# Attention with a cached key and value, and a gated mixer: two of seven reads of a product pair on ScalarE, an interleaved order of VectorE's additions, early gating for two quarters

## The chip, the core and the metric

The kernel runs on one core of one Trainium2 chip. A core has five engines that run their own instruction streams in order: TensorE (PE in the profile, with PEld for its weight loads), VectorE (DVE), ScalarE (ACT), GpSimd (POOL) and SyncE (SP), which here issues nearly all DMAs. The engines wait for one another with semaphores. The metric is the time of one execution on the device in microseconds (us); less is better.

## What is computed

The reference layer-normalises `x` (2048 tokens of width 512), runs attention over a cached key and value (32 heads, 2048 keys, head width 128), runs a mixer with an MLP on the same normalised input, and combines them:

```python
xn = _layernorm(x, axis=-1)
q = (xn @ wq).reshape(B, Sq, H, Dh).transpose(0, 2, 1, 3)
scores = jnp.einsum("bhqd,bhkd->bhqk", q, k_cache) * (Dh ** -0.5)
p = _softmax(scores, axis=-1)
s = jnp.einsum("bhqk,bhkd->bhqd", p, v_cache).transpose(0, 2, 1, 3).reshape(B, Sq, H * Dh) @ wo
...
g = _silu(_B_ref(xn, w1, w2, w3, w4))
return x + s * g
```

All inputs and the output are bfloat16. `_B_ref` is a layer norm, a 512x512 product with gelu, a shift of the four column quarters along the tokens, a second 512x512 product added to its input, and an MLP of width 1792.

## The kernel before, in words

A first stage (about 120 us) computes layer norms, the mixer and most of the MLP, and leaves the gate `g` (twice silu's value) in the tile `xall`, 128 tokens by 512 per block. The rest is attention, and the change is all in there.

Attention is cut into 128 units. A unit is one head and one quarter of 512 query tokens; the order is group of four heads (8 groups, `g`), then quarter (`qt`, 4), then head in the group (`hh`, 4). A unit `u` has eight slots (`p` = 0 to 7), so the loop at the end of the function runs over slots `n = 8u + p`, and everything that any engine does is put into a slot by hand; the order of the calls is the order on each engine. In each slot

- `s_slot` makes two score matmuls of 128x512 into one of two PSUM tiles `ps_s`, and one exp of 128x1024 on ScalarE into `pT` (L416);
- `pv_run` makes two matmuls of probabilities and values of the slot ten slots back into `ps_o` (two PSUM banks, one for each unit);
- further matmuls make the query projection of later units (`q_mm` or `product`) and the output projection of earlier ones (`wo_mm` into `ps_wo`, one token block of 128 for about each unit).

The softmax sums need the probabilities of a unit added up over all keys. VectorE does that in bf16: `add_first` (L422) and two `add_next` (L427) add four tiles of 128x2048 into `acc`; `fold` (L431) and `fold_last` (L435) fold it to 128x512. Then `turn` (L460) transposes it with a DMA into `tT`, `turned_sums` reduces it (L465, `sm`) and takes the reciprocal (L467, `rc`), a 2 KB DMA writes that to DRAM (L469, `dr`), `bcast` (L473) reads it back to all partitions with a 256 KB DMA (`rb`), and `norm` (L485) multiplies `ps_o` by `rb` into `oT`, which the output projection reads. In slot terms: the last `add_next` of unit `u-1`, its folds, and `turned_sums` of unit `u-2` stand at `p = 0` of unit `u`; `bcast(u-2)` at `p = 1`; `turn(u-1)` at `p = 3`; `norm(u-2)` at `p = 7`. So the write of `dr` and the read of `rb` for unit `u-2` lie between `p = 0` and `p = 7` of the same unit `u`.

The query projection of units 16 to 125 goes by pairs of heads with a scheme of Strassen's kind: 7 products of half-size blocks (`product`, two matmuls of 128x256 each) in place of 8, put into one PSUM tile `ps_q` with two sides. Products 1, 6 and 2 fill it first; then the same buffer (there is one) takes products 7, 5, 4 and 3. `q_part` takes the results out in four steps, which read PSUM seven times in all: step 0 copies side 0 to `m1` (L388) and adds side 1 to it (L389, `u`); step 1 copies side 0 into the query tile (L392); step 2 adds (L397, then L398, which needs L397's result); step 3 adds `u` to both sides (L400). All are on VectorE. They stand at slots 3, 6, 11 and 14 of 16.

`wo_post` adds a block of the output projection to its sum `sacc` (L549). In the last group the sum is multiplied by the gate (L558) and the input is added (L560). For the last quarter (`LATE = (QT - 1,)`) that is done in advance: once the block's sum of group `GY - 1` is there, `fin_load` loads the input block, `y_scale` (L515) multiplies the sum by the gate, and `y_add` (L520) adds the input, one unit apart; a block that comes later, in group `GY` or after, is multiplied by the gate by itself (`tm`) and added.

On SP's queue all DMAs are issued in program order, and an issue that has to wait (for `dr` to have landed, for example) holds up those behind it.

Of the kernel before, what the change touches and what calls it, by code (L numbers as in the profile page):

```python
# [8 lines left out]
ACT = mybir.ActivationFunctionType  # L9
ALU = mybir.AluOpType  # L10
FP32 = mybir.dt.float32
BF16 = mybir.dt.bfloat16
# [5 lines left out]
def kernel(  # L18
# [15 lines left out]
    nc = tc.nc  # L34
    P = nc.NUM_PARTITIONS
# [9 lines left out]
    QT = Sq // 512  # L45
# [6 lines left out]
    NG = H // HG  # L52
# [9 lines left out]
    pin = tc.keep_in_program_order  # L62
# [28 lines left out]
    qp2 = ent(pool("qp2", 2))  # L91
    smp = ent(pool("smp", 4))
# [18 lines left out]
    def mm(out, lhsT, rhs, start, stop, **kw):  # L111
# [9 lines left out]
        out=ident[:], in0=diag[:], scalar1=0.0, scalar2=None, op0=ALU.is_equal))  # L121
# [1 line left out]
    HEAD = 7  # L123
    XS = 3 * QT + 1
    units = [(g, qt, hh) for g in range(NG) for qt in range(QT) for hh in range(HG)]
    LATE = (QT - 1,)
    GY = NG - 1
    NU = len(units)
    TURN = range(NU - HG)
    NS = NU * SPU  # L130
    kTs, vBs, wqs, wos, oTs, st = {}, {}, {}, {}, {}, {}
# [202 lines left out]
    sw = {}  # L334
# [28 lines left out]
    def product(v, k):  # L363
# [16 lines left out]
        for dc in range(2):  # L380
            mm(s["ps"][:, side, :], b[:, dc, :], x[:, dc, :], k in (1, 7) and dc == 0, True, skip_group_check=True)

    def q_part(v, i):
        s = sw[v]
        ps, t = s["ps"], lambda: pS.tile([P, 256], FP32, tag="tq", bufs=3, name="tq")
        if i == 0:
            m1, s["u"] = t(), t()
            pin(nc.vector.tensor_copy(out=m1[:], in_=ps[:, 0, :]))  # L388
            pin(nc.vector.tensor_tensor(out=s["u"][:], in0=ps[:, 1, :], in1=m1[:], op=ALU.add))  # L389
        elif i == 1:  # L390
            q = s["q"] = qp2.tile([P, 4, 256], BF16, name="qT")
            pin(nc.vector.tensor_copy(out=q[:, 0, :], in_=ps[:, 0, :]))  # L392
            for j in range(2):
                st[v + j] = dict(qT=q[:, 2 * j:2 * j + 2, :].rearrange("d a b -> d (a b)"))
        elif i == 2:
            u3 = t()
            pin(nc.vector.tensor_tensor(out=u3[:], in0=ps[:, 0, :], in1=s["u"][:], op=ALU.add))  # L397
            pin(nc.vector.tensor_tensor(out=s["q"][:, 3, :], in0=ps[:, 1, :], in1=u3[:], op=ALU.add))  # L398
        else:
            pin(nc.vector.tensor_tensor(  # L400
                out=s["q"][:, 1:3, :], in0=ps[:], in1=s["u"][:].unsqueeze(1).to_broadcast([P, 2, 256]),
                op=ALU.add))
            del sw[v]
# [21 lines left out]
    def add_next(u, i):  # L425
        a = st[u]["acc"]
        pin(nc.vector.tensor_tensor(out=a[:], in0=a[:], in1=st[u]["pT"][i][:], op=ALU.add))  # L427

    def fold(u):
        a = st[u]["acc"]  # L430
        pin(nc.vector.tensor_tensor(out=a[:, 0:2, :], in0=a[:, 0:2, :], in1=a[:, 2:4, :], op=ALU.add))  # L431

    def fold_last(u):
        a = st[u]["acc"]
        pin(nc.vector.tensor_tensor(out=a[:, 0, :], in0=a[:, 0, :], in1=a[:, 1, :], op=ALU.add))  # L435
# [25 lines left out]

    def turned_sums(u):
        s = st[u]
        sm = smp.tile([P, 4], FP32, name="sm")
        pin(nc.vector.tensor_reduce(out=sm[:], in_=s["tT"][:], axis=mybir.AxisListType.X, op=ALU.add))  # L465
        rc = smp.tile([P, 4], FP32, name="rc")
        pin(nc.vector.reciprocal(out=rc[:], in_=sm[:]))  # L467
        s["dr"] = drp.tile([P, 4], FP32, name="dr")
        pin(nc.sync.dma_start(out=s["dr"][:], in_=rc[:]))  # L469
# [190 lines left out]
    for jc in range(DC):  # L660
        b = BASE_J[jc]
# [150 lines left out]
    pS = None  # L812
    for h in range(HG):
        load_wo(h)
    for g in range(NG - 1):
        b = (g * QT + QT - 1) * HG
# [45 lines left out]
    UA, UB = NU - 2, NU - 1  # L862
# [14 lines left out]
    steps = defaultdict(list)  # L877
    for v in pairs:
        a = (v - 2) * SPU
        for k, n in ((1, 1), (6, 2), (2, 5), (7, 8), (5, 9), (4, 12), (3, 13)):  # L880
            steps[a + n].append((product, v, k))
        for i, n in enumerate((3, 6, 11, 14)):
            steps[a + n].append((q_part, v, i))

    def run_steps(n, which):
        for fn, v, k in steps.get(n, ()):
            if fn is which:
                fn(v, k)
# [4 lines left out]
    for h in range(HG, H, 2):  # L893
        u = (h // HG) * QT * HG + (-4, -2)[h % HG // 2]
# [8 lines left out]
    for n in range(UB * SPU):  # L903
        u, p = divmod(n, SPU)
        extra = len(wo_todo) > 1 and u in (2 * HG, 2 * HG + 1)
        if p == 0 and wo_box:
            wo_slot(4, n, each=1)
        s_slot(u, p)
        pv_run(n)
        for v, dcs in q_plan.get(n, ()):  # L910
            q_mm(v, dcs)
        run_steps(n, product)
        if p == 0 and u - 2 in TURN:
            turned_sums(u - 2)
        if p == 1 and u - 2 in TURN:
            bcast(u - 2)
        if p == 0 and 1 <= u:
            add_next(u - 1, 3)
            fold(u - 1)
            if u != UA:  # L920
                fold_last(u - 1)
        if p == 3 and u - 1 in TURN:
            turn(u - 1)
        if p == 0:
            twice = extra
        if twice and p < 3:
            wo_slot(p, n, tag="xa")
        for v, k in ((u + 1, 3), (u + 2, 7)):
            if p == k and "psq" in st.get(v, ()) and (k == 3) == (v > FIRST):
                q_copy(v)  # L930
        if p == 3:
            run_steps(n, q_part)
        if u - 2 in TURN:
            norm_p, sum_p, wo_p, each = 7, 5, 3, 1
        else:
            norm_p, sum_p, wo_p, each = 4, 5, 4, 1
        at_wo = [wo_p + i for i in range(HG // each + 1)]
        if FIRST - 2 <= u < LAST:
            at_wo = ([0, 3, 4, 6, 7], [0, 2, 3, 6, 7], [3, 4, 5, 6, 7], [0, 2, 3, 6, 7])[u % 4]
        if p == norm_p and 2 <= u and not u - 2 in TURN:  # L940
            norm_queue(u - 2)
        if p == sum_p and 1 <= u and u - 1 not in TURN:
            sums(u - 1)
        if p == sum_p + 1 and 1 <= u and u - 1 not in TURN:
            bcast(u - 1)
        if u == UA and p in (1, 2, 3):
            wo_slot(p - 1, n)
            if p == 3:
                fold_last(u - 1)
        if p in at_wo and wo_todo and pS is not None and (p == at_wo[0] or wo_box):  # L950
            wo_slot(at_wo.index(p), n, each=each)
        if p == norm_p and u - 2 in TURN:
            norm_queue(u - 2)
        if p != 3:
            run_steps(n, q_part)
        if p == 4:
            add_first(u)
        if p == 6:
            add_next(u, 2)
        pay()  # L960
        held_mm(n)
        for fn in todo.pop(n, ()):
            fn()
        if pS is None and not held:
            right.close()
            pS = right.enter_context(pool("pS", side="right", reuse_waits="tile"))
# [3 lines left out]
    n = UB * SPU  # L970
# [156 lines left out]
```

## Time and profile before

| | |
|---|---|
| median of 3 runs | 1246.01 us (1244.84 to 1246.2) |
| profiled execution, its own time | 1244.64 us |
| its span, first to last instruction | 1242.8 us |
| busy: PE, DVE, ACT | 1230.5, 1081.4, 1092.2 us |
| granted TensorE clock | 1.00 |

A row of a group reads: line, engine, operation, out<-in by the program's names, shapes, count, then busy time, mean ns of one, and the idle time of the engine just before these instructions with what ended it. A row of the timeline reads: start, duration, engine, line, operation, names, count, and in brackets the idle time before it. SPq is SP's queue, whose rows are DMA issues. A busy share of PE is not proof that PE runs at its peak, since matmuls are pipelined and overlap; starts that follow at the least distance are.

### The profile page before, as it was taken

Reading aid. Unit: us, or ns where it says so; the run is one execution under the profiler, and the core shown is the slowest. Engines: PE = TensorE matmul, PEld = TensorE weight load, DVE = VectorE, ACT = ScalarE, POOL = GpSimd, SP = SyncE. Lnnn points to the kernel's source line nnn. Section 1 sums busy time; section 2 is a strip of 40 time slices with the busy share of each in tenths; the row PEclk is TensorE's granted clock in tenths of the full one; section 3 lists DMA queues with packets and bytes.
Section 4 is the critical chain, followed back from the end, with each engine's and each line's share of the span. In section 5 each row is a group of like instructions: output and inputs, shape, how many; then the busy total and the mean of one; then the engine's idle time right before and its main releaser. Section 6 shows DMA issues by size and latency. Waiting matters only on the chain.

```text
span 1242.8 us, 17421 instructions
## 1 busy us (share of the span) xinstructions
PE 1230.5 (99%) x6267; PEld 645.0 (52%) x6267; DVE 1081.4 (87%) x1745; ACT 1092.2 (88%) x1127; POOL 26.8 (2%) x75
## 2 busy tenths in 40 slices
PE   9999999999999999999999999999999999999898
PEld 7444444455555555555555555555555555555445
DVE  7712778899999999999999999999999999999997
ACT  6345999899999999999999999999999999999886
POOL 5300000000000000000000000000000000000000
PEclk9999999999999999999999999999999999999999
DMA  7660123554334524443244423453354433563322
GB/s 176 169 138 31 30 39 65 100 97 88 69 73 106 108 47 85 91 111 77 63 96 98 94 60 82 94 117 61 66 103 94 90 69 74 104 114 68 68 73 82
DMA packets 244055, 107.74 MB, mean 87 GB/s; under 512 B 194816, under 2 KB 227712, under 8 KB 243968
## 3 DMA queue, kind: packets, MB, share of 16 engines
q1 hardware_dynamic: 243408, 106.17, 40.9%
q8 instruction: 49, 0.80, 0.3%
q10 hardware_dynamic: 560, 0.46, 0.1%
q14 instruction: 38, 0.31, 0.1%
HBM read 67.50 MB, written 2.36 MB: 56 GB/s over the span
## 4 chain that ended last, share of the span: by engine, by line
PE 86%; DVE 11%; DMA 2%; ACT 1%; issue 1%; SPq 0%; DVEq 0%; ACTq 0%
PE ps_s L112 35%; PE ps_o L112 33%; PE ps_q L112 7%; PE ps_wo L112 7%; DVE acc L427 3%; PE ps_m L112 2%; DVE oT L485 1%; DVE acc L431 1%; DMA rb<-dr 1%; DVE sm L465 1%; ACT pT L416 1%; DVE sacc L549 1%; DVE xall L558 1%; DVE acc L422 1%; DVE acc L435 1%
## 5 line engine op out<-in xcount | busy, mean ns | idle before, releaser
L416 ACT ACTIVATE pT<-ps_s 128x1024 bf16<-128x1024 f32 x1016 | 1019.7, 1024 | 77.0 <-PE ps_s L112 41.6
L112 PE MATMUL ps_s<-qT,kT 128*128 128x512 bf16 (+1 forms) x2064 | 609.1, 377 | 0.0
L112 PE MATMUL ps_o<-pT,vb 128*128 128x512 bf16 x1984 | 589.9, 379 | 0.0
L427 DVE TENSOR_TENSOR acc<-acc,pT 128x2048 bf16<-128x2048 bf16 x254 | 306.9, 1208 | 11.5 <-ACT pT L416 11.2
L112 PEld LDWEIGHTS <-kT 128*128 128x128 bf16 x2064 | 232.9, 113 | 147.3 <-issue 2.1
L112 PEld LDWEIGHTS <-vb 128*128 128x128 bf16 x1984 | 193.9, 98 | 216.9 <-issue 0.3
L112 PE MATMUL ps_wo<-wo_h,oT 128*128 128x512 bf16 x496 | 186.2, 379 | 0.1
L422 DVE TENSOR_TENSOR acc<-pT 128x2048 bf16<-128x2048 bf16 x127 | 154.8, 1219 | 20.4 <-ACT pT L416 20.1
L431 DVE TENSOR_TENSOR acc<-acc 128x1024 bf16<-128x1024 bf16 x127 | 87.9, 692 | 4.3
L485 DVE TENSOR_TENSOR oT<-ps_o,rb 128x512 bf16<-128x512 f32 x127 | 86.7, 683 | 1.8 <-DMA rb<-dr 1.5
L112 PEld LDWEIGHTS <-oT 128*128 128x128 bf16 x528 | 59.1, 112 | 49.5 <-issue 0.6
L465 DVE TENSOR_REDUCE sm<-tT 128x4 f32<-128x512 bf16 x124 | 84.0, 678 | 0.7 <-DMA tT<-acc 0.7
L549 DVE TENSOR_TENSOR sacc<-ps_wo,sacc 128x512 f32<-128x512 f32 x108 | 73.9, 685 | 0.3 <-PE ps_wo L112 0.3
L112 PEld LDWEIGHTS <-wc 128*128 128x128 bf16 x440 | 43.0, 98 | 58.4 <-issue 8.1
L112 PEld LDWEIGHTS <-wq_h 128*128 128x128 bf16 x398 | 38.9, 98 | 47.9 <-issue 1.8
L112 PE MATMUL ps_q<-xnT,wq_h 128*128 128x256 bf16 (+1 forms) x288 | 61.1, 298 | 1.6 <-DVE tq L389 1.3
L400 DVE TENSOR_TENSOR qT<-ps_q,tq 128x512 bf16<-128x512 f32 x55 | 38.1, 692 | 25.4 <-PE ps_q L112 25.1
L435 DVE TENSOR_TENSOR acc<-acc 128x512 bf16<-128x512 bf16 x127 | 54.0, 425 | 4.3
L293 ACT ACTIVATE h2T<-ps_s 128x1024 bf16<-128x1024 f32 x28 | 28.7, 1025 | 25.9 <-PE ps_s L112 25.9
L112 PEld LDWEIGHTS <-w_sb 128*128 128x128 bf16 x368 | 33.7, 98 | 29.5
L112 PE MATMUL ps_s<-xn2T,w_sb 128*128 128x512 bf16 x224 | 48.8, 379 | 0.0
L112 PE MATMUL ps_q<-xs,wc 128*128 128x256 bf16 x246 | 47.0, 273 | 0.0
(99 smaller groups left out, 574.9 us busy)
## 6 DMA issues: line engine op xcount, KB each, us to landing
rb<-dr SPq DMA_DIRECT2D x127, 256.0 KB, 3.9
vb<-in_A_v_cache_dram SPq DMA_DIRECT2D x62, 256.0 KB, 3.0
wq_h<-in_A_wq_dram SPq DMA_DIRECT2D x32, 128.0 KB, 3.1
wo_h<-in_A_wo_dram SPq DMA_DIRECT2D x32, 128.0 KB, 2.9
w_sb<-in_B_w_dram SPq DMA_DIRECT2D x8, 256.0 KB, 5.0
kT<-in_A_k_cache_dram SPq DMA_TRANSPOSE x128, 2.8
xl<-in_A_x_dram SPq DMA_DIRECT2D x16, 128.0 KB, 2.5
dr<-rc SPq DMA_DIRECT2D x127, 2.0 KB, 1.4
```

The costliest lines, as they stand in the source:

```text
L112: pin(nc.tensor.matmul(out=out, lhsT=lhsT, rhs=rhs, start=start, stop=stop, **kw))
L293: pin(nc.scalar.activation(out=h2[c, f][:], in_=ps[:], func=ACT.Gelu_apprx_tanh))
L400: pin(nc.vector.tensor_tensor(out=s["q"][:, 1:3, :], in0=ps[:], in1=s["u"][:].unsqueeze(1).to_broadcast([P, 2, 256]), op=ALU.add))
L416: pin(nc.scalar.activation(out=s["pT"][-1][:, jj:jj + 2, :], in_=sps[:], func=ACT.Exp, scale=SCALE))
L422: pin(nc.vector.tensor_tensor(out=s["acc"][:], in0=s["pT"][0][:], in1=s["pT"][1][:], op=ALU.add))
L427: pin(nc.vector.tensor_tensor(out=a[:], in0=a[:], in1=st[u]["pT"][i][:], op=ALU.add))
L431: pin(nc.vector.tensor_tensor(out=a[:, 0:2, :], in0=a[:, 0:2, :], in1=a[:, 2:4, :], op=ALU.add))
L435: pin(nc.vector.tensor_tensor(out=a[:, 0, :], in0=a[:, 0, :], in1=a[:, 1, :], op=ALU.add))
L465: pin(nc.vector.tensor_reduce(out=sm[:], in_=s["tT"][:], axis=mybir.AxisListType.X, op=ALU.add))
L485: pin(nc.vector.tensor_tensor(out=to, in0=o, in1=rb, op=ALU.mult))
L549: pin(nc.vector.tensor_tensor(out=sa, in0=ps[:], in1=sa, op=ALU.add))
L558: pin(nc.vector.scalar_tensor_tensor(out=gl, in0=sa, scalar=0.5, in1=gl, op0=ALU.mult, op1=ALU.mult))
```

## The change

1. `LATE` becomes the last two quarters and `GY` goes from 7 to 6. `y_scale` and `y_add` run for the 8 blocks of quarters 2 and 3, after group 5 (before: for the 4 blocks of quarter 3, after group 6). The same 8 blocks of group 6 are gated by themselves and added to the sum (`tm`, then `sacc`: two instructions where one, L549, stood), and in group 7 they take the path of `tm` and `y_out` in place of L549, L558 and L560 (before: quarter 3 alone did).
2. The two copies of a product pair (`m1` and the first query block) go to ScalarE (`q_take`), at slots 1 and 5 of 16, right after the product that they read. VectorE's dependent pair L397, L398 is split over slots 10 and 11.
3. At `p = 0` VectorE's order was `sm`, `rc` (unit `u-2`), `add_next`, `fold`, `fold_last` (unit `u-1`). It becomes `add_next`, `sm`, `fold`, `rc`; `fold_last` moves to `p = 2`.

The instructions of PE and their order stay as they are. On SP's queue the kinds of DMA stay too; the loads of input blocks for the two quarters move to earlier units, each behind a `dr` write and ahead of the `rb` read that follows it.

```diff
-    LATE = (QT - 1,)
-    GY = NG - 1
+    LATE = (QT - 2, QT - 1)
+    GY = NG - 2
...
+    def q_take(v, i):
+        s = sw[v]
+        if i == 0:
+            s["m1"] = pS.tile([P, 256], FP32, tag="tq", bufs=3, name="tq")
+            out = s["m1"][:]
+        else:
+            q = s["q"] = qp2.tile([P, 4, 256], BF16, name="qT")
+            for j in range(2):
+                st[v + j] = dict(qT=q[:, 2 * j:2 * j + 2, :].rearrange("d a b -> d (a b)"))
+            out = q[:, 0, :]
+        pin(nc.scalar.activation(out=out, in_=s["ps"][:, 0, :], func=ACT.Identity))
+
     def q_part(v, i):
...
         if i == 0:
-            m1, s["u"] = t(), t()
-            pin(nc.vector.tensor_copy(out=m1[:], in_=ps[:, 0, :]))
-            pin(nc.vector.tensor_tensor(out=s["u"][:], in0=ps[:, 1, :], in1=m1[:], op=ALU.add))
+            s["u"] = t()
+            pin(nc.vector.tensor_tensor(out=s["u"][:], in0=ps[:, 1, :], in1=s["m1"][:], op=ALU.add))
         elif i == 1:
-            q = s["q"] = qp2.tile([P, 4, 256], BF16, name="qT")
-            pin(nc.vector.tensor_copy(out=q[:, 0, :], in_=ps[:, 0, :]))
-            for j in range(2):
-                st[v + j] = dict(qT=q[:, 2 * j:2 * j + 2, :].rearrange("d a b -> d (a b)"))
+            s["u3"] = t()
+            pin(nc.vector.tensor_tensor(out=s["u3"][:], in0=ps[:, 0, :], in1=s["u"][:], op=ALU.add))
         elif i == 2:
-            u3 = t()
-            pin(nc.vector.tensor_tensor(out=u3[:], in0=ps[:, 0, :], in1=s["u"][:], op=ALU.add))
-            pin(nc.vector.tensor_tensor(out=s["q"][:, 3, :], in0=ps[:, 1, :], in1=u3[:], op=ALU.add))
+            pin(nc.vector.tensor_tensor(out=s["q"][:, 3, :], in0=ps[:, 1, :], in1=s["u3"][:], op=ALU.add))
...
     def turned_sums(u):
         s = st[u]
-        sm = smp.tile([P, 4], FP32, name="sm")
+        sm = s["sm"] = smp.tile([P, 4], FP32, name="sm")
         pin(nc.vector.tensor_reduce(out=sm[:], in_=s["tT"][:], axis=mybir.AxisListType.X, op=ALU.add))
+
+    def turned_recip(u):
+        s = st[u]
+        sm = s["sm"]
         rc = smp.tile([P, 4], FP32, name="rc")
         pin(nc.vector.reciprocal(out=rc[:], in_=sm[:]))
...
-        for i, n in enumerate((3, 6, 11, 14)):
+        for i, n in enumerate((1, 5)):
+            steps[a + n].append((q_take, v, i))
+        for i, n in enumerate((3, 10, 11, 14)):
             steps[a + n].append((q_part, v, i))
...
         run_steps(n, product)
-        if p == 0 and u - 2 in TURN:
-            turned_sums(u - 2)
+        run_steps(n, q_take)
+        if p == 0 and 1 <= u:
+            add_next(u - 1, 3)
+            if u - 2 in TURN:
+                turned_sums(u - 2)
+            fold(u - 1)
+            if u - 2 in TURN:
+                turned_recip(u - 2)
         if p == 1 and u - 2 in TURN:
             bcast(u - 2)
-        if p == 0 and 1 <= u:
-            add_next(u - 1, 3)
-            fold(u - 1)
-            if u != UA:
-                fold_last(u - 1)
+        if p == 2:
+            run_steps(n, q_part)
+        if p == 2 and 1 <= u and u != UB and u - 1 != UA - 1:
+            fold_last(u - 1)
         if p == 3 and u - 1 in TURN:
             turn(u - 1)
...
-        if p != 3:
+        if p not in (2, 3):
             run_steps(n, q_part)
```

## The prediction

> **What bounds the kernel now.** I read the page's busy times first, then the busy times by stretch, then starts on PE and ScalarE in the steady stretch.
>
> ```profile
> PE 1230.5 (99%) x6267; PEld 645.0 (52%) x6267; DVE 1081.4 (87%) x1745; ACT 1092.2 (88%) x1127; POOL 26.8 (2%) x75
> core 0: us, PE busy (x) PEld busy (x) DVE busy (x) ACT busy (x) POOL busy (x), PEclk, DMA share, GB/s
> 196.00:283.00 87.00, 86.28 (x411) 43.06 (x410) 78.09 (x124) 78.06 (x80) 0.00 (x0) 1.00 0.50 92
> 283.00:1102.00 819.00, 819.00 (x4125) 432.08 (x4124) 764.03 (x1208) 770.75 (x768) 0.00 (x0) 1.00 0.41 86
> 1102.00:1195.00 93.00, 87.06 (x434) 45.25 (x433) 88.49 (x141) 80.76 (x81) 0.00 (x0) 1.00 0.41 77
> ```
>
> ScalarE makes eight exps for a unit, so its counts give the units: 10 units at 8.70 us in the first row, 96 at 819/96 = 8.53 in the second, some 10 at 9.3 in the third. PE is idle only in the third, for 93.0 - 87.1 = 5.9 us. That busy PE of the second row is also at its pace:
>
> ```profile
> 705.90 0.59 PE L112 MATMUL ps_s<-qT,kT 128*128 128x512 bf16 x2
> 706.33 0.59 PE L112 MATMUL ps_o<-pT,vb 128*128 128x512 bf16 x2
> 706.76 0.38 PE L112 MATMUL ps_q<-xs,wq_h 128*128 128x256 bf16 x2
> 706.98 0.59 PE L112 MATMUL ps_s<-qT,kT 128*128 128x512 bf16 x2
> 702.21 16.85 ACT L416 ACTIVATE pT<-ps_s 128x1024 bf16<-128x1024 f32 x16 [0.22 <-PE ps_s L112]
> 719.28 13.55 ACT L416 ACTIVATE pT<-ps_s 128x1024 bf16<-128x1024 f32 x13 [0.22 <-PE ps_s L112]
> ```
>
> Two matmuls of 512 columns take 0.43 from start to start, two of 256 take 0.22. A pair of units has 72 of the long (32 scores, 32 values, 8 output projection) and 14 of the short: 72 x 0.215 + 14 x 0.11 = 17.0, against 719.28 - 702.21 = 17.07 for the sixteen exps of a pair. So in the steady stretch PE sets the time, and nothing that relieves VectorE or ScalarE can gain there. In the third stretch PE waits for VectorE:
>
> ```profile
> PE ps_q L112 <- DVE qT L398: 4.5, 4, 1.7
> L558 DVE SCALAR_TENSOR_TENSOR xall<-sacc,xall 128x512 bf16<-128x512 f32 x5 | 3.5, 692 | 0.2
> L515 DVE SCALAR_TENSOR_TENSOR sacc<-sacc,xall 128x512 f32<-128x512 f32 x4 | 2.7, 685 | 0.0
> ```
>
> There the gating of the last two groups meets on VectorE, which has no idle time worth the name. These 5.9 us are all that the change can win.
>
> **The change part by part.** First VectorE's order, since its instructions hang on DMAs. One unit of before, VectorE and SP's queue:
>
> ```profile
> 844.44 1.22 DVE L427 TENSOR_TENSOR acc<-acc,pT 128x2048 bf16<-128x2048 bf16 x1
> 845.57 0.69 DVE L549 TENSOR_TENSOR sacc<-ps_wo,sacc 128x512 f32<-128x512 f32 x1
> 846.17 0.68 DVE L485 TENSOR_TENSOR oT<-ps_o,rb 128x512 bf16<-128x512 f32 x1
> 846.77 0.68 DVE L465 TENSOR_REDUCE sm<-tT 128x4 f32<-128x512 bf16 x1
> 847.48 0.18 DVE L467 RECIPROCAL rc<-sm 128x4 f32<-128x4 f32 x1
> 847.58 1.20 DVE L427 TENSOR_TENSOR acc<-acc,pT 128x2048 bf16<-128x2048 bf16 x1
> 848.81 0.69 DVE L431 TENSOR_TENSOR acc<-acc 128x1024 bf16<-128x1024 bf16 x1
> 849.54 0.42 DVE L435 TENSOR_TENSOR acc<-acc 128x512 bf16<-128x512 bf16 x1
> 847.69 0.32 SPq L469 DMA_DIRECT2D dr<-rc  x1
> 849.09 0.32 SPq L473 DMA_DIRECT2D rb<-dr  x1
> 849.99 1.21 SPq L460 DMA_TRANSPOSE tT<-acc  x1
> ```
>
> An instruction that does not need the one before it starts before that one's end: L549 1.13 after the L427 that lasts 1.22, L465 0.60 after L485. One that does need it starts later: L431 1.23 after L427, L467 0.71 after L465, L435 0.73 after L431. The difference is about 0.11 (1.23 - 1.13, and 0.71 - 0.60), and the new order takes it away three times a unit and twice a pair more (m1 then u, L397 then L398). [...]
>
> Now the circle that this order closes. `norm` (L485) of a unit waits for `rb`; behind `norm`, in VectorE's order, stands the `rc` of the next unit; behind `rc` stand `dr` and `rb` of that unit; and its `norm` waits for these. Once round is one unit, so it must fit into 8.53. Its DMA legs in the steady stretch (who waited for whom on SP's queue, then from issue to landing for the instructions of L473, then VectorE's wait):
>
> ```profile
> SPq L473 <- DMA dr<-rc: 135.3, 96, 2.8
> DMA to landing us min/median/max: 3.1/3.9/5.6
> DVE oT L485 <- DMA rb<-dr: 0.5, 1, 0.5
> ```
>
> SP issues `dr` (0.32), waits 135.3/96 = 1.41 on the mean for its landing, and `rb` lands 3.9 (median) after its issue: 5.63. Before, round the circle: `norm` 0.60, `sm` 0.71, `rc` 0.18, 0.03 to the issue (847.66 to 847.69), 5.63, in all 7.15. That leaves 8.53 - 7.15 = 1.38 of room, and so `norm` waited for `rb` once in 96 units (last row). After, `add_next` and `fold` stand between `norm` and `rc`: `norm` 0.60, `add_next` 1.13, `sm` 0.60, `fold` 0.60 (as the other 0.69 instruction, L549), `rc` 0.18, 0.03, in all 3.14; with 5.63 that is 8.77. The order costs 1.62 on the circle and saves 0.11 in it; the room was 1.38. It no longer fits, by 8.77 - 8.53 = 0.24 a unit. VectorE cannot save up time for it, as `add_next` needs the unit's last exp. So VectorE falls behind a little each unit until PE waits, at L398's data or at the `ps_o` bank that `norm` frees, and then PE keeps the circle's pace. I expect about 1 us of falling behind before PE feels it, an estimate: in the unit at 704 us L398 ended at 705.04 and the product behind it began at 705.68, and L398 comes some 0.35 sooner in the new order.
>
> ```profile
> 704.62 0.42 DVE L398 TENSOR_TENSOR qT<-ps_q,tq 128x256 bf16<-128x256 f32 x1
> 705.68 0.38 PE L112 MATMUL ps_q<-xnT,wc 128*128 128x256 bf16 x2
> ```
>
> Nothing else on VectorE lengthens the circle: what stands between `rc` and `norm` (fold_last, up to three steps of a pair, two big additions, sacc) is 0.34 x 3 + 0.60 + 2 x 1.13 + 0.60 = 4.5 from start to start (0.42 less 0.08 for the short ones), and lies beside the 5.63 of the DMAs. The transpose of `tT`, which waited for L435 until 849.99, now stands right behind `rb`, 0.5 sooner; `sm`, which needs it, comes 1.73 behind a `norm` that waits for `rb` itself, so it is in time, but its packets run beside `rb`'s a little longer. The loads behind it (kT, vb, wo, wq) move with it.
>
> The copies. VectorE loses two a pair, near 0.42 each:
>
> ```profile
> L388 DVE COPY tq<-ps_q 128x256 f32<-128x256 f32 x48 | 20.0, 418 | 0.0
> L400 DVE TENSOR_TENSOR qT<-ps_q,tq 128x512 bf16<-128x512 f32 x48 | 33.2, 692 | 23.1 <-PE ps_q L112 23.0
> L609 ACT ACTIVATE oT<-ps_t 128x256 bf16<-128x256 f32 x2 | 0.8, 384 | 0.4 <-PE ps_t L112 0.4
> 125.21 4.98 ACT L416 ACTIVATE pT<-ps_s 128x1024 bf16<-128x1024 f32 x5
> 130.09 0.62 ACT L306 ACTIVATE th<-xall 128x512 bf16<-128x512 bf16 x1
> ```
>
> L400 alone waits 23 us for PE in the steady stretch, so VectorE has room there and the loss of the copies is worth nothing. On ScalarE one costs between 0 (hidden) and 0.384 (L609, the same size). Back to back an exp takes (130.09 - 125.21)/5 = 0.98, so a pair needs 16 x 0.98 + 2 x 0.384 = 16.4 of 17.07: I take 0 for the time. Queued behind a copy is the next exp, 0.38 later at most, which two `ps_s` buffers cover; without that cover 55 pairs x 0.77 = 42 us.
>
> The gating. `y_scale`, `y_add` and `tm` (0.60 each, as L549) move into units 94 to 117, one a unit, between `rc` and `norm`: 4.5 + 0.6 = 5.1 still lies beside 5.63, also with two more instructions in group 7 (5.4). They cost nothing while the circle is longer; at most 0.6 a unit for 24 units, 14 us, if VectorE were full. The overload of the third stretch goes, and its units fall to the circle's 8.77.
>
> The sum, on the profiled execution's 1244.64 us (span 1242.8 and 1.84 around it; the median of the runs is 1.4 above): 96 x 0.24 = +23.0; the ten units of the first row 10 x 0.07 = +0.7; the ten of the third 87.7 - 93.0 = -5.3; falling behind -1.0. That is 1262.
>
> **The rivals.**
> The circle fits. With the medians (from issue to landing 1.4 for the instructions of L469, in the row below, and 3.9 for `rb`) its DMA legs are 5.3 and it is 8.44, below 8.53; that half of the units are like that speaks for it, and that the late ones are never made up speaks against it, since the break-even of the mean is 5.39 and the mean is 5.63. Then only the end changes: 1244.6 - 5.3 = 1239.
>
> ```profile
> DMA to landing us min/median/max: 1.4/1.4/3.2
> ```
>
> The Trainium skill's page DMA: Bandwidth & Descriptors, section Anatomy of one DMA, puts a DMA at about 2.0 us and its bytes over 436 GB/s, most of the fixed part being the write's receipt; by that `rb` would be an estimated 2.6 and `dr` 2.0, and the circle would fit. The trace has 3.1 as the least for `rb`.
>
> The circle runs at its slow end. SP's queue shows stretches where `dr` took 2.7 and 3.2:
>
> ```profile
> 352.27 0.34 SPq L469 DMA_DIRECT2D dr<-rc  x1
> 354.98 0.34 SPq L473 DMA_DIRECT2D rb<-dr  x1
> 360.28 0.32 SPq L469 DMA_DIRECT2D dr<-rc  x1
> 363.51 0.32 SPq L473 DMA_DIRECT2D rb<-dr  x1
> ```
>
> With 2.7 and 3.2 (near `rb`'s least) the legs are 5.9 and a unit 9.04: 96 x 0.51 + 10 x 0.34 - 2.6 - 1 = +49, 1293. For it: the loads now follow `rb` sooner. Against: such stretches are a minority, as the mean of 1.41 shows.
>
> [...]
>
> ScalarE's copies hold up the exps: up to +42, 1288; against it the 16.4 of 17.07.
>
> The circle is over 8.53, but so little that the end's gain pays for it: at 8.62 a unit, 96 x 0.09 - 10 x 0.08 - 10 x 0.68 - 1 = 0, so 1245, no change.
>
> **How the numbers follow.** Chances: the forecast's mechanism with a unit of 8.65 to 8.95 0.67; the circle fits or misses by under 0.07 0.15; no change (8.60 to 8.65) 0.07; slow end 0.08; ScalarE 0.02; no overlap 0.01. The likeliest gives 1262; its own ends are 1248 (8.65) and 1283 (8.95), worked out as the sum. The range adds the no-change case and the near misses below it, down to a unit of 8.59, and leaves out the circle that fits (0.10) and what lies above 8.95: 1242 to 1283. Faster than before by over 0.2% 0.15, within 0.2% (2.5 us, about what a measurement of this kernel can tell) 0.07, slower 0.78.
>
> **What would show it.** Right: VectorE's L496 (`norm`) idle before it, released by DMA `rb`, in most units, 20 us or more in all; exps of a pair some 17.5 apart; PE waits spread over the steady stretch, at `ps_q` or `ps_o`; SP waiting for `rc` later in the unit. Wrong: `norm` without waits and pairs at 17.07, or PE's waits released by ScalarE. Should `dr` and `rb` together land within 5.39 on the mean, the forecast falls to the first rival.

## The result, and the profile after

| | before | changed |
|---|---|---|
| median of 4 runs each, same chip | 1245.42 us (1244.59 to 1246.2) | 1273.18 us (1271.38 to 1274.18) |
| profiled execution, its own time | 1244.64 us | 1274.15 us |
| its span | 1242.8 us | 1272.4 us |

The changed kernel takes 1.0221 times the time of the kernel before (95% interval 1.0204 to 1.0239): it is slower by 27.8 us. The forecast was 1262 us, in a range of 1242 to 1283, so the measured time lies in the range and 11 us above the forecast.

The page of the changed kernel first, busy times and then the chain that ended last:

```profile
PE 1236.0 (97%) x6147; PEld 644.3 (51%) x6267; DVE 1018.4 (80%) x1647; ACT 1112.2 (87%) x1237; POOL 26.9 (2%) x75
DMA 37%; PE 30%; DVE 25%; issue 6%; ACT 2%; DVEq 0%; SPq 0%; ACTq 0%
DMA rb<-dr 24%; PE ps_s L112 12%; DMA dr<-rc 11%; DVE acc L434 10%; PE ps_o L112 10%; DVE acc L438 5%; DVE sm L472 4%; PE ps_q L112 3%; DMA tT<-acc 3%; PE ps_m L112 2%; ACT pT L423 2%; PE ps_wo L112 1%; DVE oT L496 1%; DVE rc L478 1%; DVE acc L442 1%
```

VectorE has lost 63 us of work (1081.4 before), and the kernel is slower. Of the 63, 110 copies at 0.42 are 46; the rest was not taken apart. No engine is full: PE's 97% is 2 points below before, and a busy PE is not a PE at its pace. The chain says what took over. Its two largest DMA shares are `rb<-dr` and `dr<-rc`, 35% together, and the VectorE lines in it (L434 `add_next`, L472 `sm`, L438 `fold`, L478 `rc`, L496 `norm`) are those of the circle.

The steady stretch of the changed kernel, 283 to 1102 us, in the view of who waited for whom (total, times, longest), and the idle row of `norm` over the whole span from the page's groups:

```profile
DVE oT L496 <- DMA rb<-dr: 85.9, 88, 2.0
PE ps_q L112 <- DVE qT L405: 18.3, 32, 1.4
PE ps_o L112 <- DVE oT L496: 1.5, 4, 0.5
L496 DVE TENSOR_TENSOR oT<-ps_o,rb 128x512 bf16<-128x512 f32 x127 | 87.7, 691 | 96.0 <-DMA rb<-dr 95.5
```

`norm` waited for `rb` once in this stretch before, for 0.5 us; now it waits in 88 of its 93 instances, 85.9 us in all. PE's waits are spread over the stretch (the 32 for L405 begin at 297 us and go on to 1097) and end with VectorE's L405 (L398 before), a few with `norm`.

How long is a unit now? The instructions of `norm` in that stretch, one a unit, with their count and the starts of the first and the last, of the kernel before and then of the changed one:

```profile
L485 DVE TENSOR_TENSOR oT<-ps_o,rb x96: 681/682/692, 282.5 to 1093.7; 128x512 bf16<-128x512 f32 x96
```

```profile
L496 DVE TENSOR_TENSOR oT<-ps_o,rb x93: 681/692/693, 284.2 to 1101.3; 128x512 bf16<-128x512 f32 x93
```

(1093.7 - 282.5)/95 = 8.54 before, (1101.3 - 284.2)/92 = 8.88 after: 0.34 more for each of 96 units, 32.6 us. That is more than the whole difference of the spans, 29.6; the rest of the program gave about 3.0 back.

Once round the circle in the changed kernel, VectorE and then SP's queue from the timeline:

```profile
806.32 0.69 DVE L496 TENSOR_TENSOR oT<-ps_o,rb 128x512 bf16<-128x512 f32 x1 [0.87 <-DMA rb<-dr]
806.93 1.22 DVE L434 TENSOR_TENSOR acc<-acc,pT 128x2048 bf16<-128x2048 bf16 x1
808.06 0.68 DVE L472 TENSOR_REDUCE sm<-tT 128x4 f32<-128x512 bf16 x1
808.65 0.68 DVE L438 TENSOR_TENSOR acc<-acc 128x1024 bf16<-128x1024 bf16 x1
809.25 0.17 DVE L478 RECIPROCAL rc<-sm 128x4 f32<-128x4 f32 x1
...
815.06 0.69 DVE L496 TENSOR_TENSOR oT<-ps_o,rb 128x512 bf16<-128x512 f32 x1 [0.28 <-DMA rb<-dr]
...
809.45 0.34 SPq L480 DMA_DIRECT2D dr<-rc  x1
810.87 0.34 SPq L484 DMA_DIRECT2D rb<-dr  x1
```

`norm` starts when `rb` lands. From there 0.61, 1.13, 0.59, 0.60 and 0.17 to the end of `rc`, 0.03 to the issue of `dr`: 3.13, where 3.14 was forecast. The starts show the overlap that the forecast took from the trace of before: `sm` 1.13 behind an `add_next` that lasts 1.22, `fold` 0.59 behind a `sm` of 0.68. The Trainium skill's page VectorE: DVE Perf Modes (The DRAIN you can't avoid) says that the next instruction starts when the pipe has emptied, and adds that one that is not held starts earlier. The trace agrees with what it adds: both starts just named come before the end of the instruction ahead. Then 815.06 - 809.45 = 5.61 pass until `rb` is there and the next `norm` starts, 8.74 after the first. Before the change `dr` was issued 1.52 behind `norm` (847.69 - 846.17 in the trace of before); here it is 3.13. On the mean of the stretch the DMA legs are longer than 5.61. SP's wait for `dr`, and the time from issue to landing of L484:

```profile
SPq L484 <- DMA dr<-rc: 118.2, 92, 2.6
DMA to landing us min/median/max: 3.2/4.1/5.9
```

0.32 + 118.2/92 + 4.1 = 5.70, where the trace of before gave 5.63. So the circle by these rows is 3.14 + 5.70 = 8.84, beside a measured unit of 8.88.

### The profile page after: what moved, and what is told of

The parts are those of the page before. It is cut to its first block, busy times and chain, and to the rows that moved or that the text cites. A ratio compares the mean times of both kernels' runs of the same rounds, so it can differ in the third digit from the quotient of the medians.

```text
span 1272.4 us, 17526 instructions
## 1 busy us (share of the span) xinstructions
PE 1236.0 (97%) x6147; PEld 644.3 (51%) x6267; DVE 1018.4 (80%) x1647; ACT 1112.2 (87%) x1237; POOL 26.9 (2%) x75
## 4 chain that ended last, share of the span: by engine, by line
DMA 37%; PE 30%; DVE 25%; issue 6%; ACT 2%; DVEq 0%; SPq 0%; ACTq 0%
DMA rb<-dr 24%; PE ps_s L112 12%; DMA dr<-rc 11%; DVE acc L434 10%; PE ps_o L112 10%; DVE acc L438 5%; DVE sm L472 4%; PE ps_q L112 3%; DMA tT<-acc 3%; PE ps_m L112 2%; ACT pT L423 2%; PE ps_wo L112 1%; DVE oT L496 1%; DVE rc L478 1%; DVE acc L442 1%
## 5 line engine op out<-in xcount | busy, mean ns | idle before, releaser
L112 PE MATMUL ps_s<-qT,kT 128*128 128x512 bf16 (+1 forms) x2020 | 599.4, 377 | 0.9
L112 PE MATMUL ps_o<-pT,vb 128*128 128x512 bf16 x1936 | 579.5, 379 | 6.4 <-DVE oT L496 2.4
L434 DVE TENSOR_TENSOR acc<-acc,pT 128x2048 bf16<-128x2048 bf16 x254 | 309.5, 1218 | 47.3 <-ACT pT L423 46.8
L112 PE MATMUL ps_wo<-wo_h,oT 128*128 128x512 bf16 x482 | 181.2, 379 | 0.3
L496 DVE TENSOR_TENSOR oT<-ps_o,rb 128x512 bf16<-128x512 f32 x127 | 87.7, 691 | 96.0 <-DMA rb<-dr 95.5
L438 DVE TENSOR_TENSOR acc<-acc 128x1024 bf16<-128x1024 bf16 x127 | 86.5, 681 | 0.1
L472 DVE TENSOR_REDUCE sm<-tT 128x4 f32<-128x512 bf16 x124 | 84.2, 679 | 1.7 <-DMA tT<-acc 1.7
L560 DVE TENSOR_TENSOR sacc<-ps_wo,sacc 128x512 f32<-128x512 f32 x96 | 65.6, 684 | 0.0
L112 PE MATMUL ps_q<-xnT,wc 128*128 128x256 bf16 x194 | 36.9, 271 | 21.8 <-DVE qT L405 21.6
```

The costliest lines, as they stand in the source:

```text
L112: pin(nc.tensor.matmul(out=out, lhsT=lhsT, rhs=rhs, start=start, stop=stop, **kw))
L496: pin(nc.vector.tensor_tensor(out=to, in0=o, in1=rb, op=ALU.mult))
L560: pin(nc.vector.tensor_tensor(out=sa, in0=ps[:], in1=sa, op=ALU.add))
```

## The experiments

Theory, as in the prediction: `rc` behind `add_next` and `fold` makes the circle longer than PE's 8.53 us, and the unit becomes the circle. Rivals: the loss comes from ScalarE's copies, or from the gating in the steady stretch, or from the splitting of VectorE's steps; and, for the size, that something beside the circle holds up the DMAs. Each experiment's ratio is to the kernel before, run on the same chip. There were three chips, one for every four experiments; the kernel before had medians of 1246.52, 1246.34 and 1246.45 on them, in the order in which they follow here: sums first, order alone, copies alone and gating alone on the first; the changed kernel again and the three other orders on the second; the last four on the third.

**One part undone: the sums before the additions again.** From the changed kernel, only the order at `p = 0`:

```diff
-            add_next(u - 1, 3)
             if u - 2 in TURN:
                 turned_sums(u - 2)
-            fold(u - 1)
             if u - 2 in TURN:
                 turned_recip(u - 2)
+            add_next(u - 1, 3)
+            fold(u - 1)
```

> The changed kernel with one thing undone: at p = 0 sm and rc (unit u-2) stand ahead of add_next and fold again; the copies on ScalarE, the early gating and fold_last at p = 2 stay. Circle theory (norm, sm, rc, dr, rb, norm must fit into PE's 8.53 us a unit): the circle is 0.60 + 0.71 + 0.18 + 0.03 + 5.75 = 7.27, room 1.26, so norm waits for rb in fewer than 10 units, a pair of units takes 17.07 again, and only the end differs from before: 1237 to 1241. Rival, the copies hold up the exps on ScalarE: they are still there, so it stays at 1262 or more. Rival, the gating's instructions fill VectorE: units 94 to 117 stay over 8.8, 1250 or more.

1245.03 us (1244.25 to 1246.37), ratio 0.9988 (0.9978 to 0.9997). Its waits and its `norm` in the steady stretch:

```profile
DVE oT L496 <- DMA rb<-dr: 1.3, 2, 0.9
L496 DVE TENSOR_TENSOR oT<-ps_o,rb x95: 679/681/692, 289.9 to 1101.1; 128x512 bf16<-128x512 f32 x95
```

The wait for `rb` is gone and so is the loss. All copies, splits and gating are still in this kernel, so without the new order at `p = 0` they don't cost the 28 us. A unit takes (1101.1 - 289.9)/94 = 8.63, which is still 0.09 more than before. But the time is some 4 us above what was expected: something in it takes back the gain at the end. The last group of experiments looks for that.

**One part alone: the order.** The kernel before with `add_next`, `sm`, `fold`, `rc` at `p = 0` and `fold_last` at `p = 2`; copies and gating as before:

```diff
-        if p == 0 and u - 2 in TURN:
-            turned_sums(u - 2)
...
+            add_next(u - 1, 3)
+            if u - 2 in TURN:
+                turned_sums(u - 2)
+            fold(u - 1)
+            if u - 2 in TURN:
+                turned_recip(u - 2)
```

> The kernel before with the new order alone (add_next, sm, fold, rc at p = 0, fold_last at p = 2); copies on VectorE, gating as before. Circle theory: units take 8.85 to 8.9 in the steady stretch as in the changed kernel, +30 to +34 there, and the end keeps its overload: 1272 to 1282. Both rivals (copies on ScalarE, gating): neither is in it, so 1243 to 1248.

1298.07 us (1297.77 to 1299.6), ratio 1.0412 (1.0395 to 1.043): the order alone costs more than the whole change had cost. Waits, `norm`, SP's wait and the landing of `rb` in its steady stretch:

```profile
DVE oT L489 <- DMA rb<-dr: 94.8, 90, 3.0
PE ps_q L112 <- DVE qT L398: 28.6, 42, 1.2
L489 DVE TENSOR_TENSOR oT<-ps_o,rb x91: 691/692/693, 284.6 to 1099.7; 128x512 bf16<-128x512 f32 x91
SPq L477 <- DMA dr<-rc: 116.8, 90, 2.9
DMA to landing us min/median/max: 3.2/4.2/6.1
```

A unit takes (1099.7 - 284.6)/90 = 9.06, and its legs are 0.32 + 116.8/90 + 4.2 = 5.82. The signature is the changed kernel's; the size is larger than expected, and the legs are longer (5.82 against 5.70). Either the copies and the gating shorten the circle, or the DMAs are slower here than when the changed kernel was first measured. So it had to be run again.

**The changed kernel, unaltered, once more.**

> The changed kernel once more, beside its variants on one chip. The DMA legs (from rc's end to rb's landing) were 5.73 on the mean in its first profile, 5.9 in the profiles of the first four experiments, the unaltered-order ones too. Circle theory: a unit is 3.13 + the leg + 0.02 or 0.03, so with legs of 5.7 to 5.95 units of 8.85 to 9.1 and 1270 to 1297, following the leg of this chip by 10 us of time for each 0.1 us. Rival (the leg does not set the pace, something else in the new order does): 1273 whatever the leg is.

1295.38 us (1294.76 to 1295.5), ratio 1.0395 (1.0377 to 1.0412). The same rows:

```profile
DVE oT L496 <- DMA rb<-dr: 110.8, 90, 2.7
L496 DVE TENSOR_TENSOR oT<-ps_o,rb x91: 679/691/693, 284.6 to 1101.7; 128x512 bf16<-128x512 f32 x91
SPq L484 <- DMA dr<-rc: 115.9, 90, 2.7
DMA to landing us min/median/max: 3.2/4.3/6.1
```

The same program is 22 us slower than in its first measurement, while the kernel before differs by less than 1 us (1246.34 against 1245.42). Its legs are 0.32 + 115.9/90 + 4.3 = 5.91, which is 0.21 more than in its first profile, and its unit is (1101.7 - 284.6)/90 = 9.08, 0.20 more. 0.20 in some 110 units is the 22 us. The unit is also within 0.02 of the one with the order alone (9.06), so the copies and the gating don't shorten the circle. Both parts of the theory show in this: the unit follows the DMA legs one to one once the circle is over, and not at all while it isn't.

**Other lengths of the same circle.** All three are the first experiment's kernel with only `add_next` and `fold` moved past the sums. The copies, the gating and `fold_last` at `p = 2` stay.

```diff
 order on VectorE at p = 0
-first experiment:   sm, rc, add_next, fold
+recip late:         sm, add_next, rc, fold
+add first:          add_next, sm, rc, fold
+both first:         add_next, fold, sm, rc
```

By the starts that the prediction lists, the part on VectorE is 0.60 + 0.60 + 1.13 + 0.18 + 0.03 = 2.54 for the first of them, 0.60 + 1.13 + 0.71 + 0.21 = 2.65 for the second and 0.60 + 1.23 + 0.60 + 0.71 + 0.21 = 3.35 for the third. With the 5.91 that the changed kernel showed on this chip the circles are 8.45, 8.56 and 9.26, against PE's 8.53: one just under, one just over, one far over.

> The changed kernel with the order sm, add_next, rc, fold at p = 0: the reduction and its reciprocal still have another instruction between them. The circle is 0.60 + 0.60 + 1.13 + 0.18 + 0.03 + 0.03 = 2.57 and the leg of 5.7 to 5.95: 8.27 to 8.52, just under PE's 8.55. Circle theory: as fast as e1_sums_first, 1243 to 1248. Rival (any order that parts sm and rc holds things up, by the interleaving itself): 1255 or more.

> The changed kernel with the order add_next, sm, rc, fold: only add_next is ahead of sm, and rc follows sm directly. The circle is 0.60 + 1.13 + 0.71 + 0.18 + 0.03 + 0.03 = 2.68 and the leg: 8.38 to 8.63, at the edge. Circle theory: 1243 to 1256, some norm waits for rb, far fewer than in the changed kernel. Rival (what hurts is that add_next, with its wait for an exp, stands ahead of sm): near the changed kernel's time.

> The changed kernel with the order add_next, fold, sm, rc: the circle is 0.60 + 1.23 + 0.60 + 0.71 + 0.18 + 0.06 = 3.38 and the leg, 0.22 longer than in the changed kernel. Circle theory: 0.22 x 106 = 23 us more than the changed kernel on the same chip, 1295 to 1320. Rival (the cost is a fixed one of a wait, not a length of a circle): the changed kernel's time within 5 us.

1252.19 us (1250.56 to 1254.86), ratio 1.005 (1.0034 to 1.0066); 1251.26 us (1250.9 to 1251.75), ratio 1.0041 (1.0026 to 1.0055); 1326.82 us (1324.8 to 1327.13), ratio 1.0643 (1.0627 to 1.0659). The first came out above what its theory expected (1243 to 1248), the second within it, the third above it (1295 to 1320): it is 31 us over the changed kernel on the same chip, where the theory had 23 and the rival at most 5. No rival's time came out. The wait for `rb` and `norm` in the steady stretch, one kernel after the other:

```profile
DVE oT L496 <- DMA rb<-dr: 16.9, 30, 1.8
L496 DVE TENSOR_TENSOR oT<-ps_o,rb x94: 677/690/693, 290.4 to 1098.9; 128x512 bf16<-128x512 f32 x94
```

```profile
DVE oT L496 <- DMA rb<-dr: 23.9, 42, 2.1
L496 DVE TENSOR_TENSOR oT<-ps_o,rb x94: 677/691/693, 290.6 to 1098.8; 128x512 bf16<-128x512 f32 x94
```

```profile
DVE oT L496 <- DMA rb<-dr: 120.1, 87, 3.4
L496 DVE TENSOR_TENSOR oT<-ps_o,rb x88: 681/691/693, 288.1 to 1099.3; 128x512 bf16<-128x512 f32 x88
```

| order at `p = 0` | circle by rows | unit measured | waits of `norm` for `rb` | time less before |
|---|---|---|---|---|
| sums first (its own trace: 1.55 + 5.90) | 7.45 | 8.63 | 1.3 us | -1.5 us |
| recip late | 8.45 | (1098.9 - 290.4)/93 = 8.69 | 16.9 us | +5.9 us |
| add first | 8.56 | (1098.8 - 290.6)/93 = 8.69 | 23.9 us | +4.9 us |
| changed kernel, this chip | 9.05 | 9.08 | 110.8 us | +49.0 us |
| both first | 9.26 | (1099.3 - 288.1)/87 = 9.32 | 120.1 us | +80.5 us |

Far over the limit the unit is the circle by these rows to within 0.06 (0.10 for the order alone: 3.14 + 5.82 = 8.96, 9.06 measured). What is left comes from the median in the sum. Taken unit by unit from the traces, as means of the stretch, the way from `norm` to the issue of the next `dr`, from there to the landing of `rb`, and from the landing to the next `norm` are 3.16 + 5.70 + 0.03 in the changed kernel at first, 3.14 + 5.89 + 0.02 with the order alone, 3.15 + 5.90 + 0.02 in the changed kernel again and 3.39 + 5.91 + 0.03 with both first. The last term is what the circle leaves over: 0.02 to 0.03 says that `norm` starts when `rb` lands. It is 1.37 in the kernel before and 1.18 with the sums first, where the circle costs nothing. Between, recip late has 2.59 + 5.91 + 0.19 and add first 2.67 + 5.91 + 0.11: their circles nearly fill the unit on the mean, some are late (30 and 42 of 94), and a unit that fits doesn't make up for one that didn't. Their 8.69 has to be held against the 8.63 of the sums first, which has the same copies and gating, and not against PE's 8.53; so what the circle costs them is some 0.06 a unit. The prediction's first rival went by the medians; a circle of 2.59 + 5.91 = 8.50 fits into 8.53 and is still late 30 times.

**One part alone: the copies, and the gating.**

```diff
...
+        pin(nc.scalar.activation(out=out, in_=s["ps"][:, 0, :], func=ACT.Identity))
...
-        for i, n in enumerate((3, 6, 11, 14)):
+        for i, n in enumerate((1, 5)):
+            steps[a + n].append((q_take, v, i))
+        for i, n in enumerate((3, 10, 11, 14)):
```

> The kernel before with the two copies of a pair on ScalarE and the pair's two dependent additions split, the order at p = 0 and the gating as before. Circle theory: no cost in the steady stretch (17.07 a pair), VectorE less full at the end: 1239 to 1244. Rival, copies hold up the exps: 55 pairs at up to 0.77, PE waits at ps_s or ps_o, 1255 to 1288.

1248.11 us (1247.37 to 1250.42), ratio 1.0014 (1.0005 to 1.0023).

```diff
-    LATE = (QT - 1,)
-    GY = NG - 1
+    LATE = (QT - 2, QT - 1)
+    GY = NG - 2
```

> The kernel before with the early gating for two quarters alone. Circle theory: VectorE has some 0.8 us of idle time a pair in the steady stretch, the gating adds 1.2 a pair in units 94 to 117, so it spreads part of the end's 5.9 us of PE idle over earlier units: 1240 to 1247. Rival, the gating fills VectorE: 1250 to 1260.

1249.33 us (1247.53 to 1251.81), ratio 1.0023 (1.0013 to 1.0032). Both came out slower, where each was expected to gain or to be level. They had been costed at nothing. For the gating the waits view of its steady stretch names the price, a row that the kernel before doesn't have there:

```profile
PE ps_q L112 <- DVE qT L398: 5.3, 6, 1.6
```

VectorE was busy for 764 of 819 us there before, so 0.57 was free in a unit; a step of 0.60 more in each of the last units, ahead of L398, is about what is free. Five of the six waits, 4.2 of the 5.3 us, come after 945 us, where the gating begins; one, at 383 us, does not belong to it. By the starts of the exps, eight for a unit, units 114 and on take 124.8 us in place of 127.9, but the 96 units ahead of them 828.4 in place of 820.0. So, while VectorE carries the copies, the early gating gives less at the end than it costs ahead of it.

For the copies there is another row. How often a weight load of PE stood without a named releaser in the steady stretch, before, and then with the sums first (copies on ScalarE):

```profile
PEld L112 <- issue: 2.2, 13, 0.2
```

```profile
PEld L112 <- issue: 15.6, 62, 1.5
```

62 - 13 = 49 more, in a stretch of 48 pairs: once a pair. The place is in the timeline, before and then with the sums first:

```profile
471.91 0.59 PE L112 MATMUL ps_s<-qT,kT 128*128 128x512 bf16 x2
472.34 0.59 PE L112 MATMUL ps_o<-pT,vb 128*128 128x512 bf16 x2
472.56 0.31 PEld L112 LDWEIGHTS <-wc 128*128 128x128 bf16 x2
472.77 0.38 PE L112 MATMUL ps_q<-xs,wc 128*128 128x256 bf16 x2
```

```profile
472.55 0.59 PE L112 MATMUL ps_o<-pT,vb 128*128 128x512 bf16 x2
472.59 0.38 ACT L393 ACTIVATE tq<-ps_q 128x256 f32<-128x256 f32 x1
472.77 0.10 PEld L112 LDWEIGHTS <-wc 128*128 128x128 bf16 x1
473.02 0.38 PE L112 MATMUL ps_q<-xs,wc 128*128 128x256 bf16 x2
473.02 0.10 PEld L112 LDWEIGHTS <-wc 128*128 128x128 bf16 x1 [0.16 <-issue]
```

`ps_q<-xs,wc` at this place is product 6. Before, it starts 0.43 behind the matmuls ahead of it, at PE's pace; now 0.47, and its second weight load, which was done in advance, waits until 473.02. ScalarE's copy of `m1` ends at 472.97. Product 6 writes side 1 of the tile whose side 0 the copy reads, so it doesn't need the copy's result, but the two touch the same PSUM tile, and in the trace product 6 waits for ScalarE's semaphore: in all 48 pairs of the stretch it starts 0.05 behind the end of the copy, and by the distances of the starts on PE some 4.4 us are lost there in all. Whether the program could leave this wait out was not tried. If it is the cost, product 6 ahead of the copy ends it.

**Product 6 ahead of the copy.** From the first experiment's kernel, with the sums first:

```diff
-        for k, n in ((1, 1), (6, 2), (2, 5), (7, 8), (5, 9), (4, 12), (3, 13)):
+        for k, n in ((1, 1), (6, 1), (2, 5), (7, 8), (5, 9), (4, 12), (3, 13)):
```

> e1_sums_first with product 6 moved from slot 2 into slot 1, right behind product 1, so that it is issued ahead of the copy on ScalarE that reads the other side of ps_q. In e1_sums_first a pair takes 17.10 to 17.18 where the kernel before has 17.07 to 17.14, and 5.2 us of PE's surplus lies between ps_o and ps_q<-xs,wc. Theory A (product 6 waits for the copy's read of the same PSUM tile): the surplus goes to under 1 us, pairs at 17.07, 1239 to 1243. Theory B (ScalarE's own time, two copies of 0.38 a pair, holds up the exps): no change, 1244 to 1247.

1241.26 us (1240.69 to 1241.37), ratio 0.9961 (0.9947 to 0.9975). **The copy of `m1` back on VectorE**, with product 6 in its old place:

```diff
-            s["u"] = t()
+            s["m1"], s["u"] = t(), t()
+            pin(nc.vector.tensor_copy(out=s["m1"][:], in_=ps[:, 0, :]))
...
-        for i, n in enumerate((1, 5)):
-            steps[a + n].append((q_take, v, i))
+        steps[a + 5].append((q_take, v, 1))
```

> e1_sums_first with the first copy (m1) back on VectorE in front of the addition that needs it; the second stays on ScalarE. Theory A (product 6 waits for the first copy): PE's surplus at ps_q<-xs,wc goes as in e9_six_with_one, pairs at 17.07; VectorE is 0.45 a pair fuller, which shows in units 94 to 124 alone: 1240 to 1245. Theory B (ScalarE's time): half of the surplus stays, 1243 to 1246.

1243.34 us (1242.29 to 1245.21), ratio 0.9976 (0.9967 to 0.9985). PE's weight loads in the steady stretch, first with product 6 ahead, then with one copy:

```profile
PEld L112 <- issue: 6.0, 14, 1.7
```

```profile
PEld L112 <- issue: 7.3, 16, 1.6
```

The waits are gone either way, 48 of them with product 6 ahead (62 to 14) and 46 with one copy (62 to 16). Product 6 ahead of the copy is worth 0.9988 - 0.9961 = 0.0027, 3.4 us, and the intervals lie apart, if only just (the two ran on different chips, each beside its own kernel before). Both copies are still on ScalarE there, so it is this wait that costs, and not ScalarE's time. The time with one copy, 1243.34, lies in the ranges of both theories; there the waits decide, and they are gone. That it gives less fits VectorE's extra 0.42 a pair, but the intervals of the two overlap.

**Is the early gating worth anything then?** From the kernel with product 6 ahead: first the gating as before, then only `LATE` as before, with `GY` still a group earlier.

```diff
-    LATE = (QT - 2, QT - 1)
-    GY = NG - 2
+    LATE = (QT - 1,)
+    GY = NG - 1
```

```diff
-    LATE = (QT - 2, QT - 1)
+    LATE = (QT - 1,)
```

> e9_six_with_one with LATE and GY as in the kernel before (gating of one quarter, after group 6). Theory (VectorE has room for the end's overload once the copies are gone from it, and the gated additions of group 6 cost more than they save): PE's surplus in units 96 to 112 goes from some 3 us to under 1, the end keeps 2 to 4: 1238 to 1243, and not slower than e9_six_with_one by more than 2. Rival (the early gating is what takes the end's stall away): 1243 to 1246, slower than e9_six_with_one by 2 or more.

> e9_six_with_one with LATE of one quarter, but after group 5 (GY = NG - 2). Half of the early gating: between e9_six_with_one and e10_gate_late if each gated block costs alike, 1237 to 1242; if the stalls come from blocks that meet with weight sums (units 106 to 112), faster than both.

1242.07 us (1241.12 to 1243.07), ratio 0.9968 (0.9956 to 0.998), and 1240.28 us (1239.26 to 1240.91), ratio 0.9956 (0.9941 to 0.997). With the early gating for two quarters it was 1241.26. The three lie within 1.8 us and their intervals overlap: whatever the gating is worth, it is hardly to be seen. The traces show why: by the starts of the exps, units 18 to 113 take 823.7 us with the early gating for two quarters and 820.5 with the gating as before, and what follows takes 121.5 and 124.9; what the early gating gives at the end it costs ahead of it. The last kernel has the least median of this study, some 6 us below the kernel before and 33 to 55 below the changed one: sums first, copies on ScalarE, product 6 ahead of the copy, one quarter gated a group earlier.

## Why the prediction was right, and where it was off

- *The circle is over PE's 8.53 and sets the unit.* Right, and shown from three sides: undoing the order removes the loss, the order alone makes it, and longer and shorter circles give longer and shorter units. That the time fell into the range is in part luck: the same kernel took 1295 us in its second measurement, above the range, by DMA legs 0.2 longer.
- *VectorE's part is 3.14.* Right (3.13 in the unit above). The 0.11 that the interleaving saves in the circle is real; it is spent many times over, because `add_next` and `fold`, 1.13 + 0.60 = 1.73, then stand in it. The prediction's 1.62 is the net of the two, though it says that the 0.11 comes off it.
- *The DMA legs are 5.63.* Too small, and the main error: 5.70 in the first measurement and up to 5.91 in the experiments. Because the room was only overdrawn by 0.24, an error of 0.07 to 0.28 in the legs is large in the result. The forecast's 96 x 0.24 = 23.0 became 96 x 0.34 = 32.6. Unit by unit the 8.88 is 3.16 + 5.70 + 0.03, so of the 0.11 over 8.77 the legs are 0.07, the time from `rb`'s landing to `norm`, which the forecast left out, 0.03, and VectorE's part 0.02. The slow-end rival's 9.04 a unit is what the changed kernel came to in its second measurement (9.08, and 1295 where that rival gave 1293).
- *The end gains 5.3, the first ten units lose 0.7, falling behind gives 1.0.* In sum -5.6; measured 29.6 - 32.6 = -3.0. The same units by the starts of the exps:

| us | units 8 to 17 | 18 to 113 | 114 to 123 | from there to the last exp |
|---|---|---|---|---|
| before | 88.0 | 820.0 | 92.6 | 35.4 |
| changed | 88.9 | 852.7 | 89.7 | 34.2 |
| forecast of the difference | +0.7 | +23.0 | -5.3 | 0 |

  The first ten came out as forecast. The end is where it was off: its units were put at the circle's 8.77, took 8.97 and gained 2.9 in all. In three of these ten `norm` doesn't start when `rb` lands but 0.57 to 0.70 later, 1.9 us in all, because VectorE still has the gating of the blocks that are not done early in front of it (L569 and L571, at L558 and L560 before). One of the three, where `rb` landed at 1189.93:

```profile
1188.71 0.68 DVE L560 TENSOR_TENSOR sacc<-ps_wo,sacc 128x512 f32<-128x512 f32 x1
1189.43 0.69 DVE L569 SCALAR_TENSOR_TENSOR xall<-sacc,xall 128x512 bf16<-128x512 f32 x1
1190.16 0.42 DVE L571 TENSOR_TENSOR xl<-xall,xl 128x512 bf16<-128x512 bf16 x1
1190.50 0.68 DVE L496 TENSOR_TENSOR oT<-ps_o,rb 128x512 bf16<-128x512 f32 x1
```

  The prediction had let all that stands between `rc` and `norm` lie beside the DMA legs; here it doesn't. The 1.0 for falling behind can't be told apart in these figures. (A small slip: at 8.59 the prediction's sum gives 1241 and not 1242, the lower end of its range.)
- *The copies cost 0.* Wrong, and hidden in this kernel by the circle. What was costed was ScalarE's time and the exps behind a copy; what was left out was the matmul into the other side of the tile that the copy reads. It is 3.4 us once the circle fits.
- *The gating costs 0 while the circle is longer.* Not contradicted in the steady stretch of the changed kernel; by itself it costs about 2.8 us in place of winning 5.9.
- *The signs named beforehand.* `norm` idle until `rb`, 20 us or more: 95.5. Pairs of exps some 17.5 apart: 2 x 8.88 = 17.8. PE's waits spread at `ps_q` or `ps_o`: 18.3 and 1.5. SP waiting for `rc` later in the unit: 3.13 behind `norm`, 1.52 before. By the estimate that the prediction worked out from the Trainium skill's page DMA: Bandwidth & Descriptors (Anatomy of one DMA), 2.6 for `rb` and 2.0 for `dr`, the circle would have fitted. That section gives its figures for DMAs that GpSimd issues, and these are SP's; the 256 KB read lands 4.1 to 4.3 after its issue in the median here, and 3.2 at the least.

## What to carry to other kernels

Where an engine's order in a loop closes on itself through DMAs, add up the loop once round, with the DMAs' mean times, and hold it against the period of the engine that sets the pace: instructions moved ahead of the one that starts the DMAs cost nothing while there is room, and their full length in every round beyond it. Where the loop just fits on the mean, some rounds are late all the same (30 and 42 of 94 here). Taking away the gap behind a dependent instruction (0.11 here) is no gain where the instruction put between lengthens that loop. And when a copy out of PSUM is given to an idle engine, look for who touches the same PSUM tile next; putting that one ahead of the copy was worth 3.4 us here.

## What was not expected of the hardware

The read of 256 KB that waits for a 2 KB write landed at different times in different measurements of the same program, 4.1 against 4.3 us in the median, and with the write's landing the legs were 5.70 against 5.91. On the three chips of the experiments the legs agree: unit by unit they are 5.87 to 5.94 in all twelve kernels. Only the two profiles of the first measurement have shorter ones, 5.65 before and 5.70 changed, and on which chip that was is not on record; so whether the chip or something else made them shorter stays open. The kernel before, which has 1.4 us of room, had medians within 1.1 us of each other in all four sets of runs; the changed one has none, and took 1273 and 1295 us. The new order is not what makes the legs longer: the kernel with the gating alone has the old order and ran on the chip of the kernel with the new order alone. SP's wait and the landing of `rb` in its steady stretch:

```profile
SPq L473 <- DMA dr<-rc: 138.8, 95, 3.8
DMA to landing us min/median/max: 3.2/4.1/5.4
```

0.32 + 138.8/95 + 4.1 = 5.88, where the new order had 5.82 on that chip (unit by unit 5.87 and 5.89). So the time of a kernel whose loop has no room can differ from one set of runs to another by far more than runs within a set do: 1.0221 and 1.0395 are both right for their own set.
